# Attention with a soft mixture of experts and a gated layer: where the keys are rounded, and when the third pair's first maxima are taken

## The chip, the cores and the metric

The kernel runs on one core of one Trainium2 chip. The metric is the device time of one execution in microseconds (us). Engines are named as in the profile: PE is TensorE's matmul, PEld its weight load (which overlaps PE), DVE is VectorE, ACT is ScalarE, POOL is GpSimd, SP issues the DMAs.

## The reference, cut to what matters

```python
def _attn_ref(q, k, v):                       # q, k, v: 4 x 8 heads x 1152 x 64
    q_pool = q.reshape(B, H, S // 2, 2, D).mean(axis=3)          # 576 queries
    scores = scale * np.matmul(q_pool, k.transpose(0, 1, 3, 2))  # 576 x 1152
    scores = scores - np.max(scores, axis=-1, keepdims=True)
    attn = np.exp(scores)
    attn = attn / (np.sum(attn, axis=-1, keepdims=True) + 1e-09)
    return np.matmul(attn, v)
def reference(**kwargs):
    ...                                       # 2304 x 512 after the heads are put together
    x = _moe_ref(x=x, **moe_kwargs)           # soft mixture of 8 experts, 32 slots
    return _moe2_ref(x=x, **moe2_kwargs)      # RMS norm, gated layer of width 1536
```

The change concerns the attention alone.

## The kernel before

**Pairs.** The 32 heads are worked off as 16 pairs (`p` 0 to 15), one after the other; the two heads of a pair lie in the two halves of the 128 partitions. Everything else (experts, gated layer) comes after the last pair, apart from weights that are fetched and unpacked along the way.

**One pair.** There are 9 key tiles of 128 keys. For each, `qk` (L398) forms the scores of 288 queries in a two-bank tile `sc` in PSUM: four products per head, with keys and queries split into a rounded part and a rest (`kh`, `kl`, `qh`, `ql`), the fourth product subtracting the row maxima (`mr`). ACT takes the exponential (L409, tile `e`), POOL adds the exponentials up (`add_e`, L424, tile `acc`), and `av` (L426) multiplies them by the values. The row maxima have to be known beforehand, so they are computed one pair ahead: `max_item` (L319), for all but the first pair `wide_item` (L340), does products of the rounded parts alone into a two-bank tile `mxp`, and DVE reduces each tile to its maxima (L351, L357, L361, L364). A pair has 11 such items: 0 to 7 are four query tiles by two blocks of 512 keys, 8 takes the last 128 keys of all four query tiles, 9 and 10 take the last 64 queries. `max_red` and `max_row` then join them and turn them into a row (L374, tile `mxt`) that two DMAs per head send into `mr`.

**Visits.** Three key tiles make a visit; in its last tile (`kt % 3 == 2`) the steps `a`, `b`, `c` do the products with the values for all three tiles, and the steps `m` put maxima between them. Pair 0 does its two query halves one after the other (18 steps `u`, six visits), the others both together (9 steps, three visits).

**How many maxima.** `MAX`, `MAX_0` and `MAX_1` say how many items may be taken in each step. Pair 0 takes what is left of its own (five) and all 11 of pair 1; its last visit has none. Pair 1 takes items 0 to 8 of pair 2 and then items 0 to 2 of pair 3, 12 in all: one in its second step, four, four and three in its visits. From pair 2 on a pair takes items 3 to 8 of the next pair and 0 to 2 of the one after (`AHEAD` is 3), nine in all, three per visit. Items 9 and 10 of the next pair (`max_tail`) come in the first visit. `STEP_1` has one more `m` than `STEP_V` for pair 1's four, and `AT_P1` sets `max_red` later in pair 1.

**PSUM.** `sc`, `mxp` and the small tiles (`sums`, `sumt`, `xl`, `mxt`) take turns in three two-bank buffers. A tile can begin only when the engine that reads the last but two has done so.

**Side work.** All else is placed by the table `AT` (and `AT_0`, `AT_1`, ... for some pairs): a number is a point in the pair's 9 steps at which the function is written into the program, and each engine works through its instructions in the order in which they were written. Those of the first visit that matter here are `round_k` (L285: ACT rounds 576 keys of the pair after next, `kh` from `kraw`, whose DMA L275 is issued at the start of the pair), `abs_64` (ACT unpacks a weight, L714 and L716), `sums` (L446: PE sums up the exponentials' totals, ACT copies them to `srow`, L458), `max_tail`, and `recips` (L460: PE transposes `srow` into `sumt`, DVE takes reciprocals, L472).

Of the kernel before, what the change touches and what calls it, by code (L numbers as in the profile page):

```python
# [18 lines left out]
NP = 16  # L19
# [10 lines left out]

STEP = "q0 m q1 m e0 e1".split()
STEP_V = "q0 q1 m e0 e1 a m m b c".split()
STEP_1 = "q0 q1 m e0 e1 a m m b m c".split()
STEP_0 = "q e".split()
STEP_0V = "q e m a m m b m c".split()
VISIT = 3
PART = 5, 6
MAX = [0, 0, 3, 0, 0, 3, 0, 0, 3]
MAX_1 = [0, 1, 4, 0, 0, 4, 0, 0, 3]
NMAX = 9  # L40
AHEAD = 3
AT = dict(
    take_x=0.0,
    load_64=[0.1, 3.0, 5.0],
    load_q=0.3,
    load_k=0.31,
    spill=[1.4, 4.4],
    sum_q=2.2,
    round_k=[2.5, 5.5],
    abs_64=[2.51, 2.89, 8.5],  # L50
    sum_up=[0.1, 0.11],
    sums=2.75,
# [13 lines left out]
    max_red=5.75,  # L66
# [18 lines left out]
AT_0 = dict(  # L85
    load_v=7.3,
    round_k1=[0.6, 1.6],
    block_q1=1.62,
    low_q=2.1,
    row_0=2.97,  # L90
    low_k=[3.6, 5.1],
    load_q=4.3,
    load_k=5.73,
    sum_q=5.91,
    high_q=6.19,
    max_red=7.3,
    max_row=7.48,
    send_row=7.49,
    round_k=[7.6, 8.6],
    block_q=8.95,  # L100
)
AT_01 = dict(
    x_turn=8.85,
    x_divide=[8.86, 8.87],
    drop_x=8.88,
    d_exp=8.84,
)
AT_1 = dict(AT_01, turn_64=[0.9, 5.8, 5.81])
AT_P1 = dict(max_red=5.83)
AT_15 = dict(  # L110
    x_turn=5.8,
    x_divide=[5.81, 5.82],
# [1 line left out]
    sums_a=8.55,  # L114
    inverse_a=[8.56, 8.57],
)
MAX_0 = [0, 0, 4, 0, 0, 4, 0, 0, 3, 0, 0, 3, 0, 0, 2, 0, 0, 0]
HALVED = (0,)
SQ_DVE = (0, 2)
SP_ACT = (1, 5, 4, 3, 2)  # L120
# [28 lines left out]
def attention_softmoe_gated_kernel(ctx: ExitStack, tc: tile.TileContext, kT, qT, vv, ip, cst, w1, w2, wg, wv, wo, rg, out):  # L149
# [78 lines left out]
    def two_banks(name):  # L228
        return ps.tile([128, 2, 512], F32, tag="u", bufs=3, name=name)
# [110 lines left out]
    def wide_item(p, i):  # L340

        o = two_banks("mxp")
        q, k, m = qh[p], kh[p], mx3[p]
        heads = m[:, 0:2 * NQT].rearrange("p (s t) c -> p s t c", s=2)
        rest = slice(1024, 1152)
        if i < 8:
            t, c = divmod(i, 2)
            for s in range(2):
                r = slice(64 * s, 64 * s + 64)
                pe.matmul(o[:, s, :], lhsT=q[r, 128 * t:128 * t + 128], rhs=k[r, 512 * c:512 * c + 512], start=True, stop=True)  # L350
            dv.reduce_max(out=heads[:, :, t, c], in_=o, axis=AX.X)  # L351
        elif i == 8:
            for t in range(NQT):
                for s in range(2):
                    r = slice(64 * s, 64 * s + 64)
                    pe.matmul(o[:, s, 128 * t:128 * t + 128], lhsT=q[r, 128 * t:128 * t + 128], rhs=k[r, rest], start=True, stop=True)
            dv.reduce_max(out=heads[:, :, :, 2], in_=o.rearrange("p s (t k) -> p s t k", t=NQT), axis=AX.X)  # L357
        elif i == 9:
            for c in range(2):
                pe.matmul(o[:, c, :], lhsT=tb, rhs=k[:, 512 * c:512 * c + 512], start=True, stop=True)  # L360
            dv.reduce_max(out=m[:, 2 * NQT, 0:2], in_=o, axis=AX.X)  # L361
        else:
            pe.matmul(o[:, 0, 0:128], lhsT=tb, rhs=k[:, rest], start=True, stop=True)
            dv.reduce_max(out=m[:, 2 * NQT, 2:3], in_=o[:, 0:1, 0:128], axis=AX.X)  # L364
# [3 lines left out]
    def max_red(p):  # L368
        dv.reduce_max(out=mxw[:, 0:2 * NQT + 1], in_=mx3[p], axis=AX.X)
# [357 lines left out]
    def side(p):  # L727
        n, m, l = p + 1, p + 2, p - 1
        todo = []

        def at(name, g):
            ts = (AT_0 if p == 0 else AT_15 if p == NP - 1 else AT_P1 if p == 1 else AT if p % 4 == 3 else AT_1 if p % 4 == 1 else AT_01).get(name, AT.get(name))
            for i, t in enumerate(ts if isinstance(ts, list) else [ts]):
                todo.append((t, len(todo), (lambda i=i: g(i))))

        if p == 0:
            at("round_k1", lambda i: round_k(1, i))
            at("block_q1", lambda i: block_q(1))
            at("row_0", lambda i: (max_row(0), send_row(0, 3)))
        if n < NP:  # L740
            at("low_k", lambda i: low_k(n, slice(576 * i, 576 * i + 576)))
            at("low_q", lambda i: low_q(n))
            at("load_v", lambda i: load_v(n))
            if p:
                at("max_tail", lambda i: max_item(n, NMAX + i))
            at("max_red", lambda i: max_red(n))
            at("max_row", lambda i: max_row(n))
            at("send_row", lambda i: send_row(n))
        if m < NP:
            at("load_q", lambda i: load_q(m))  # L750
            at("load_k", lambda i: load_k(m))
            at("sum_q", lambda i: sum_q(m))
            at("high_q", lambda i: high_q(m))
            at("block_q", lambda i: block_q(m))
            at("round_k", lambda i: round_k(m, i))
        if l >= 0:
            at("take_x", lambda i: take_x(l))
            at("sum_up", lambda i: sum_up(l, 1 - i))
            at("sums", lambda i: sums(l))
            at("recips", lambda i: recips(l))  # L760
            at("x_turn", lambda i: x_turn_all(l))
            at("x_divide", lambda i: x_divide(l, range(3 * i, 3 * i + 3)))
            at("drop_x", lambda i: rel("B"))
            at("inverse", lambda i: inverse(l, i))
            at("x_logits", lambda i: x_logits(l))
            at("logit_add", lambda i: logit_add(l))
            if p % 4 == 0 and p < NP - 1:
                at("d_turn", lambda i: dpart.__setitem__(("d", l // 4), (d_turn(l // 4), d_neg(l // 4))))
                at("d_exp", lambda i: d_exp(l // 4, *dpart.pop(("d", l // 4))))
            if p % 4 == 1 and p > 1:  # L770
                b = p // 4 - 1
                at("d_back", lambda i: d_back(b))
                at("d_copy", lambda i: d_copy(b))
                at("slot_part", lambda i: slot_part(b))
                at("slot_copy", lambda i: slot_copy(b))
                at("slot_turn", lambda i: slot_turn(b, pt[:, b]))
            if p % 4 == 2 and p > 2:
                b = p // 4 - 1
                at("c_turn", lambda i: c_turn(b))
            if p % 4 == 3 and p > 3:  # L780
                b = p // 4 - 1
                at("c_exp", lambda i: c_exp(b))
                at("c_soft", lambda i: (c_sum, c_guard, c_inverse, c_out)[i](b))
        if p == 2:
            at("pair_up", lambda i: pair_up())
        if 0 < p < NP - 2:
            at("load_64", lambda i: load_64() if i < 2 or p % 2 or p < 11 else None)
            at("load_ew", lambda i: load(1, 99, KEEP_C + min(len(doubles), 4 * HELD + HELD_O)) if p >= FIRST_EW else None)
        if p < NP - 1:
            at("spill", lambda i: spill())  # L790
            at("abs_64", lambda i: abs_64(1))
            at("turn_64", lambda i: turn_64(1))
        if p == NP - 2:
            spill()
            assert not doubles
            at("load_14", lambda i: (keep_b.__setitem__(0, KEEP[3]), load(1, KEEP_A[0])))
        if p == NP - 1:
            at("sums_a", lambda i: sums(p))
            at("inverse_a", lambda i: inverse(p, i))
            at("load_15", lambda i: (keep_b.__setitem__(0, KEEP[0]), load(1, KEEP_A[1])))  # L800
        return sorted(todo, key=lambda x: x[:2])

    with tc.manual_schedule():
        q0 = qraw[0] = A([128, 2, 576], F32, "qraw")
# [46 lines left out]
        def next_max(p, mx):  # L851
            if p == 0:
                mx += 9
                if mx < 14:
                    max_item(0, mx)
                    if mx == 13:
                        max_red(0)
                else:
                    max_item(1, mx - 14)
            elif p == 1:  # L860
                max_item(2 + mx // NMAX, mx % NMAX)
            else:
                mx += AHEAD
                max_item(p + 1 + mx // NMAX, mx % NMAX)

        for p in range(NP):
            todo = side(p)
            mx = 0
            steps = [(kt, h) for h in range(2) for kt in range(NKT)] if p in HALVED else [(kt, None) for kt in range(NKT)]
            for u, (kt, h) in enumerate(steps):  # L870
                now = u / 2 if p in HALVED else u
                if kt % VISIT < VISIT - 1:
                    order = STEP if h is None else STEP_0
                else:
                    order = STEP_0V if p == 0 else STEP_1 if p == 1 else STEP_V
                quota = min(sum((MAX_0 if p == 0 else MAX_1 if p == 1 else MAX)[:u + 1]),
                            0 if p == NP - 1 else NMAX - AHEAD if p == NP - 2 else 99)
                for i, step in enumerate(order):
                    while todo and todo[0][0] <= now + i / len(order) / len(steps) * 9:
# [31 lines left out]
        for i in range(3):  # L911
            for s in range(2):
                c = slice(64 * s, 64 * s + 64)
# [196 lines left out]
        for h in range(2):  # L1110
            c = slice(256 * h, 256 * h + 256)
# [195 lines left out]
```

## Time and profile before

| | us |
|---|---|
| median of 3 runs | 722.66 (722.62 to 724.99) |
| the profiled execution | 725.93 |
| its span, first to last instruction | 723.8 |
| PE busy in the span | 692.3 (96%) |
| DVE, ACT, POOL busy | 459.5, 393.1, 435.3 |
| mean granted TensorE clock | 0.988 of full speed |

The three runs' times were taken without a profile; the rows below come from the profiled execution alone, which took 3.27 us more than their median and 2.13 us more than its own span. Busy PE includes matmuls that overlap, so it is read by stretch: how long a visit takes, and which wait stands inside it.

### The profile page before, as it was taken

What the parts mean: (1) busy time and instruction counts of PE and PEld (TensorE: products, weight loads), DVE (VectorE), ACT (ScalarE), POOL (GpSimd) and SP (SyncE); (2) the same over time, 40 slices, a digit from 0 to 9 for tenths busy, and PEclk for the clock granted to TensorE, in tenths of its full rate; (3) what the DMA queues carried; (4) which work ended last, traced back from release to release, by engine and by line L of the source; (5) the groups of instructions that cost most, each with busy time, mean ns of one, the idle gap of its engine ahead of it and who ended that gap; (6) DMA issues with size and microseconds to landing.
All of it is one profiled execution on the core that took longest, in us unless ns stands there. A gap on an engine that the chain in (4) does not pass through costs nothing.

```text
span 723.8 us, 15142 instructions
## 1 busy us (share of the span) xinstructions
PE 692.3 (96%) x5924; PEld 482.5 (67%) x5924; DVE 459.5 (63%) x663; ACT 393.1 (54%) x828; POOL 435.3 (60%) x352
## 2 busy tenths in 40 slices
PE   4998999999999999999999999879999999999998
PEld 2555676566676666666666666434467888888887
DVE  5748678887787878778878775531155755534420
ACT  2454666657657666566766545442266865554320
POOL 5585787877687867687887676230036855535320
PEclk9999999999999999999999999979999999999999
DMA  5140634834736626436427407379980100000001
GB/s 178 52 179 24 212 102 131 263 114 158 240 132 207 212 83 239 163 142 244 139 95 242 138 15 265 118 278 393 381 316 0 44 15 29 30 30 29 15 34 40
DMA packets 52854, 103.54 MB, mean 143 GB/s; under 512 B 5816, under 2 KB 19632, under 8 KB 52784
## 3 DMA queue, kind: packets, MB, share of 16 engines
q1 hardware_dynamic: 52784, 102.59, 40.9%
q8 instruction: 46, 0.75, 0.4%
q14 instruction: 24, 0.20, 0.1%
HBM read 89.39 MB, written 13.11 MB: 142 GB/s over the span
## 4 chain that ended last, share of the span: by engine, by line
PE 85%; DMA 6%; DVE 3%; ACT 3%; issue 2%; POOL 0%; SPq 0%; ACTq 0%; DVEq 0%; POOLq 0%
PE yo L1210 21%; PE sc L407 20%; PE av L430 20%; PE mxp L350 4%; PE gv L1162 4%; DMA kraw<-in_kT_dram 3%; DMA w<-away 2%; PE hin L976 2%; PE xo L492 2%; PE so L999 2%; PE xl L509 1%; PE sums L455 1%; PE mxp L360 1%; PE x L1027 1%; PE pp L569 1%
## 5 line engine op out<-in xcount | busy, mean ns | idle before, releaser
L424 POOL TENSOR_TENSOR acc<-acc,e 128x576 f32<-128x576 f32 x154 | 216.4, 1425 | 44.5 <-ACT e L409 40.3
L409 ACT ACTIVATE e<-sc 128x576 f32<-128x576 f32 x288 | 164.2, 657 | 71.0 <-PE sc L407 70.4
L351 DVE TENSOR_REDUCE mx<-mxp 128x2 f32<-128x1024 f32 x120 | 143.9, 1223 | 67.1 <-PE mxp L350 66.7
L430 PE MATMUL av<-e,vt 128*64 128x288 f32 x1152 | 168.7, 418 | 0.2 <-ACT e L409 0.2
L424 POOL TENSOR_TENSOR acc<-e 128x576 f32<-128x576 f32 x63 | 93.6, 1495 | 74.7 <-ACT e L409 74.6
L430 PEld LDWEIGHTS av<-e,vt 128*64 128x64 f32 x1152 | 72.2, 136 | 64.4 <-issue 29.6
L1210 PE MATMUL yo<-woh,hA 128*128 128x512 f32 (+1 forms) x312 | 98.9, 384 | 0.0
L407 PE MATMUL sc<-qh,kh 64*128 64x288 f32 x576 | 94.3, 324 | 1.4 <-DVE mx L351 1.0
L407 PE MATMUL sc<-mr,pick 64*128 64x288 f32 x576 | 86.6, 297 | 0.0
L407 PE MATMUL sc<-ql,kh 64*128 64x288 f32 x576 | 86.3, 296 | 0.0
L407 PE MATMUL sc<-qh,kl 64*128 64x288 f32 x576 | 86.3, 296 | 0.0
L1167 DVE SCALAR_TENSOR_TENSOR th<-th,gv 128x384 f32<-128x384 f32 x72 | 39.8, 553 | 63.0 <-ACT th L1164 62.4
L1193 POOL TENSOR_TENSOR hA<-hu,hA 128x384 fp32r<-128x384 f32 x48 | 48.7, 1016 | 42.6 <-ACT hA L1192 38.9
L407 PEld LDWEIGHTS sc<-qh,kh 64*128 64x128 f32 x576 | 55.3, 189 | 20.9 <-issue 6.6
L1210 PEld LDWEIGHTS yo<-woh,hA 128*128 128x128 f32 x312 | 57.6, 188 | 10.2 <-issue 0.7
L1164 ACT ACTIVATE th<-gv 128x384 f32<-128x384 f32 x72 | 35.2, 489 | 42.4 <-PE gv L1162 39.1
L1210 PE MATMUL yo<-wol,hA 128*128 128x512 f32 (+1 forms) x151 | 57.8, 383 | 0.0
L407 PEld LDWEIGHTS sc<-qh,kl 64*128 64x128 f32 x576 | 55.7, 190 | 0.0
L407 PEld LDWEIGHTS sc<-mr,pick 64*128 64x128 f32 x576 | 55.5, 189 | 0.0
L407 PEld LDWEIGHTS sc<-ql,kh 64*128 64x128 f32 x576 | 55.3, 188 | 0.0
L350 PE MATMUL mxp<-kh,qh 64*128 64x512 f32 x240 | 47.6, 434 | 0.0
L1169 DVE SCALAR_TENSOR_TENSOR hu<-th,gv 128x384 f32<-128x384 f32 x72 | 39.9, 554 | 8.0
(191 smaller groups left out, 1041.4 us busy)
## 6 DMA issues: line engine op xcount, KB each, us to landing
w<-in_w_dram SPq DMA_DIRECT2D x86, 256.0 KB
w<-in_w_dram SPq DMA_DIRECT2D x21, 512.0 KB
vt<-in_vv_dram SPq DMA_DIRECT2D x16, 576.0 KB
qraw<-in_qT_dram SPq DMA_DIRECT2D x15, 576.0 KB
kraw<-in_kT_dram SPq DMA_DIRECT2D x15, 576.0 KB
away<-w SPq DMA_DIRECT2D x32, 256.0 KB
w<-away SPq DMA_DIRECT2D x32, 256.0 KB
raw<-in_wg_dram SPq DMA_DIRECT2D x12, 512.0 KB
```

What stands on the lines that cost most here:

```text
L350: pe.matmul(o[:, s, :], lhsT=q[r, 128 * t:128 * t + 128], rhs=k[r, 512 * c:512 * c + 512], start=True, stop=True)
L351: dv.reduce_max(out=heads[:, :, t, c], in_=o, axis=AX.X)
L407: pe.matmul(o[:, s, 0:HQ], lhsT=w[r, wk], rhs=q[r, c], start=(i == 0), stop=(i == 3))
L409: ac.activation(ets[p, kt, h], o[:, :, 0:HQ], AF.Exp, scale=0.0625)
L424: eng.tensor_tensor(out=acc[p, h, j], in0=first[p, h, j] if n == 1 else acc[p, h, j], in1=e, op=ALU.add)
L430: pe.matmul(avt[p, h][64 * s:64 * s + 64, 0:HQ], lhsT=vt[p][:, kt, 64 * s:64 * s + 64], rhs=ets[p, kt, h][:, s], start=(kt == 0), stop=(kt ...
L1162: pe.matmul(o[i], lhsT=sg[n][:, 256 * i + 128 * c:256 * i + 128 * c + 128], rhs=cT[g], start=True, stop=True)
L1164: ac.activation(t, o[0], AF.Tanh, scale=0.5)
L1167: dv.scalar_tensor_tensor(out=t, in0=t, scalar=1.0, in1=o[0], op0=ALU.add, op1=ALU.mult)
L1169: dv.scalar_tensor_tensor(out=u, in0=t, scalar=0.5, in1=o[1], op0=ALU.mult, op1=ALU.mult)
L1193: gp.tensor_tensor(out=b, in0=u, in1=f(a), op=ALU.subtract)
L1210: pe.matmul(o, lhsT=x, rhs=w[:, c], start=(ft == 0 and i == 0), stop=(ft == NF - 1 and i == 2))
```

## The change

Three edits. First, the first half of the keys (576 of 1152) of the pair after next is no longer rounded at 2.5 of the pair's steps but at 2.88, in pairs 1 to 13: behind the first unpacked weight, the copy of the sums, `d_copy` where there is one, the two `max_tail` items and the transposes of the sums, and ahead of the second unpacked weight (2.89). Second, items 0 to 2 of pair 2 are taken in pair 0's last visit, so that pair 1 takes nine items like every later pair; `STEP_1`, `MAX_1` and `AT_P1` go, and pair 1 is placed by `AT`. Third, items 0 to 7 run over the query tiles first and the key blocks second, in all pairs, so that items 0 to 3 read keys 0 to 511 alone, which lie in the first rounded half.

```diff
-STEP_1 = "q0 q1 m e0 e1 a m m b m c".split()
-MAX_1 = [0, 1, 4, 0, 0, 4, 0, 0, 3]
-    round_k=[2.5, 5.5],
+    round_k=[2.88, 5.5],
-AT_P1 = dict(max_red=5.83)
-MAX_0 = [0, 0, 4, 0, 0, 4, 0, 0, 3, 0, 0, 3, 0, 0, 2, 0, 0, 0]
+MAX_0 = [0, 0, 4, 0, 0, 4, 0, 0, 3, 0, 0, 3, 0, 0, 2, 0, 0, 3]
         if i < 8:
-            t, c = divmod(i, 2)
+            c, t = divmod(i, 4)
...
-                    max_item(1, mx - 14)
-            elif p == 1:
-                max_item(2 + mx // NMAX, mx % NMAX)
+                    i = mx - 14
+                    max_item(1 + i // 11, i % 11)
...
-                    order = STEP_0V if p == 0 else STEP_1 if p == 1 else STEP_V
-                quota = min(sum((MAX_0 if p == 0 else MAX_1 if p == 1 else MAX)[:u + 1]),
+                    order = STEP_0V if p == 0 else STEP_V
+                quota = min(sum((MAX_0 if p == 0 else MAX)[:u + 1]),
```

ACT at the end of pair 4's first visit, before: behind the six exponentials come the rounded keys, a weight (two instructions), the copy of the sums and a second weight.

```order
L409 ACTIVATE e<-sc 128x576 x6
L289 CAST kh<-kraw 128x576
L714 ACTIVATE w_1839<-raw_1540 128x512
L716 ACTIVATE raw_1540<-raw_1540 128x512
L458 ACTIVATE srow<-sums 128x288
L714 ACTIVATE w_1874<-raw_1745 128x512
L716 ACTIVATE raw_1745<-raw_1745 128x512
L409 ACTIVATE e<-sc 128x576 x6
```

The same place now (the lines of the changed file are three lower).

```order
L406 ACTIVATE e<-sc 128x576 x6
L711 ACTIVATE w_1837<-raw_1540 128x512
L713 ACTIVATE raw_1540<-raw_1540 128x512
L455 ACTIVATE srow<-sums 128x288
L286 CAST kh<-kraw 128x576
L711 ACTIVATE w_1874<-raw_1745 128x512
L713 ACTIVATE raw_1745<-raw_1745 128x512
L406 ACTIVATE e<-sc 128x576 x6
```

The rounding has moved behind the first weight and the copy of the sums, and stands ahead of the second weight and of the next visit's exponentials.

PE from the end of pair 0 to pair 1's second step, before: the last products of scores of pair 0, six with the values, and three score tiles of pair 1 (four rows each, of which `mr,pick` is the last) with a maximum behind them.

```order
L407 MATMUL sc<-mr_82,pick_85 128x288 x2
L430 MATMUL av<-e,vt 64x288 x6
L407 MATMUL sc<-qh,kh 128x288 x2
...
L407 MATMUL sc<-mr_83,pick_84 128x288 x2
L350 MATMUL mxp<-kh,qh 128x512 x2
L407 MATMUL sc<-qh,kh 128x288 x2
```

The same place now.

```order
L404 MATMUL sc<-mr_82,pick_85 128x288 x2
L347 MATMUL mxp<-kh,qh 128x512 x2
L427 MATMUL av<-e,vt 64x288 x2
L347 MATMUL mxp<-kh,qh 128x512 x4
L427 MATMUL av<-e,vt 64x288 x4
L404 MATMUL sc<-qh,kh 128x288 x2
...
L404 MATMUL sc<-mr_83,pick_84 128x288 x2
L347 MATMUL mxp<-kh,qh 128x512 x2
```

Three maxima stand between pair 0's products with the values, and pair 1's first six score tiles follow one another without one.

## Rows read from the trace of the kernel before

**Rows 1.** The page: busy time and share of the span, by engine.
```profile
PE 692.3 (96%) x5924; PEld 482.5 (67%) x5924; DVE 459.5 (63%) x663; ACT 393.1 (54%) x828; POOL 435.3 (60%) x352
```

**Rows 2.** Stretches: start:end, length, busy us by engine, PEclk, DMA share, GB/s.
```profile
29.39:33.81 4.42, 4.42 (x43) 2.72 (x43) 3.96 (x5) 1.73 (x3) 2.78 (x2) 1.00 0.19 23
...
43.32:47.16 3.84, 3.69 (x37) 2.23 (x36) 0.00 (x0) 3.25 (x7) 2.52 (x2) 1.00 0.01 1
47.16:59.46 12.30, 10.79 (x98) 6.42 (x96) 9.01 (x11) 6.68 (x14) 8.98 (x7) 1.00 0.64 225
59.46:70.75 11.29, 9.32 (x93) 6.14 (x91) 9.16 (x11) 4.97 (x10) 6.94 (x5) 1.00 0.01 2
70.75:80.72 9.97, 9.97 (x85) 7.26 (x84) 5.36 (x7) 5.55 (x10) 6.93 (x5) 0.83 0.60 192
80.72:90.11 9.39, 9.39 (x94) 6.12 (x92) 7.05 (x10) 7.03 (x14) 6.65 (x5) 1.00 0.59 192
90.11:98.56 8.45, 8.45 (x92) 6.10 (x90) 7.02 (x11) 4.97 (x10) 6.93 (x6) 1.00 0.06 22
98.56:107.03 8.47, 8.47 (x85) 5.78 (x84) 6.73 (x9) 5.30 (x10) 8.21 (x9) 1.00 0.50 155
72.00:74.00 2.00, 2.00 (x22) 2.00 (x20) 0.00 (x0) 1.38 (x3) 1.40 (x1) 0.50 0.02 2
256.78:266.12 9.34, 9.34 (x91) 7.00 (x89) 5.34 (x8) 5.13 (x10) 6.96 (x5) 0.89 0.05 18
```

**Rows 3.** Timeline of pair 1, PEld and DVE: start, length, instruction, idle before.
```profile
51.58 0.19 PEld L407 LDWEIGHTS sc<-qh,kh 64*128 64x128 f32 x2 [1.19 <-DVE mx L351]
...
70.50 0.14 PEld L374 LDWEIGHTS mxt<-cs,mxw 128*128 128x128 f32 x1 [2.40 <-issue]
...
68.95 1.21 DVE L357 TENSOR_REDUCE mx<-mxp 128x8 f32<-128x1024 f32 x1
```

**Rows 4.** Timeline of pair 0's last visit, PEld and ACT.
```profile
45.13 0.20 PEld L430 LDWEIGHTS av<-e,vt 128*64 128x64 f32 x4 [0.16 <-issue]
...
44.72 0.67 ACT L289 CAST kh<-kraw 128x576 fp32r<-128x576 f32 x1
```

**Rows 5.** Timeline of ACT at the end of pair 4's first visit; last row pair 9's.
```profile
141.37 0.67 ACT L289 CAST kh<-kraw 128x576 fp32r<-128x576 f32 x1 [3.27 <-DMA kraw<-in_kT_dram]
...
143.06 0.40 ACT L458 ACTIVATE srow<-sums 128x288 f32<-128x288 f32 x1
...
146.13 0.65 ACT L409 ACTIVATE e<-sc 128x576 f32<-128x576 f32 x1 [1.53 <-PE sc L407]
...
285.86 0.65 ACT L409 ACTIVATE e<-sc 128x576 f32<-128x576 f32 x1 [1.44 <-PE sc L407]
```

**Rows 6.** Who waited for whom: us in total, times, longest.
```profile
ACT kh L289 <- DMA kraw<-in_kT_dram: 11.3, 6, 3.3
...
PEld mxp L363 <- ACT srow L458: 5.5, 4, 2.2
```

**Rows 7.** Timeline: item 9's reduction, next visit's first scores, pairs 4, 6, 8, 12.
```profile
141.79 1.23 DVE L361 TENSOR_REDUCE mx<-mxp 128x2 f32<-128x1024 f32 x1 [0.27 <-PE mxp L360]
...
145.23 0.19 PEld L407 LDWEIGHTS sc<-qh,kh 64*128 64x128 f32 x2 [0.44 <-DVE ql L308]
...
199.46 1.22 DVE L361 TENSOR_REDUCE mx<-mxp 128x2 f32<-128x1024 f32 x1 [0.28 <-PE mxp L360]
...
200.86 0.19 PEld L407 LDWEIGHTS sc<-qh,kh 64*128 64x128 f32 x2 [0.44 <-DVE mx L361]
...
252.75 1.23 DVE L361 TENSOR_REDUCE mx<-mxp 128x2 f32<-128x1024 f32 x1 [0.27 <-PE mxp L360]
...
256.78 0.29 PEld L407 LDWEIGHTS sc<-qh,kh 64*128 64x128 f32 x2 [0.86 <-DVE ql L308]
...
365.21 1.23 DVE L361 TENSOR_REDUCE mx<-mxp 128x2 f32<-128x1024 f32 x1 [0.27 <-PE mxp L360]
...
367.25 0.19 PEld L407 LDWEIGHTS sc<-qh,kh 64*128 64x128 f32 x2 [0.44 <-DVE rr L472]
```

More of the change, by code (lines that the diff above doesn't have):

```diff
@@ L731, in at @@
         def at(name, g):
-            ts = (AT_0 if p == 0 else AT_15 if p == NP - 1 else AT_P1 if p == 1 else AT if p % 4 == 3 else AT_1 if p % 4 == 1 else AT_01).get(name, AT.get(name))
+            ts = (AT_0 if p == 0 else AT_15 if p == NP - 1 else AT if p == 1 or p % 4 == 3 else AT_1 if p % 4 == 1 else AT_01).get(name, AT.get(name))
             for i, t in enumerate(ts if isinstance(ts, list) else [ts]):
```

## The prediction, made before the changed kernel had run

> **What bounds the kernel now.** I read the page first. PE is busy for 692.3 of 723.8 us, 96%, and no other engine comes over 67% [rows 1]: the products set the time, and the change neither adds nor removes one. It can pay only where PE stands still or runs slowly. So I read next how long each pair, and each visit in it, takes, from one visit's first weight load for scores to the next one's, and compared pairs that do the same work. Pair 1 is the odd one: its three visits take 12.30, 11.29 and 9.97 us, pair 2's take 9.39, 8.45 and 8.47 [rows 2]. That is 33.56 against 26.31 us. Pair 1 has twelve maxima items where pair 2 has nine, but its PE is busy for 10.79 and 9.32 us only in the first two visits: most of the excess is waiting.
>
> The timeline of pair 1 says for what. At 51.58 PE has waited 1.19 us for a reduction (L351) to give back a PSUM buffer: the item in pair 1's second step holds one of three buffers, and DVE comes to it late. At 70.50 PE has stood for 2.40 us ahead of the transpose of the maxima (L374), which needs the reduction of item 8; that began only at 68.95 and took 1.21 [rows 3]. Right behind this wait the granted clock is 0.50, TensorE's lower level of 1.2 GHz, and the third visit runs at 0.83 on average [rows 2]: this is why it takes 9.97 us with PE busy throughout.
>
> The list of waits shows the second place. ACT waits six times for keys in `round_k`, 11.3 us in all, and PE waits four times, 5.5 us in all, for the copy of the sums (L458) before item 10 may use its buffer (L363) [rows 6]. In pair 4 the two are one: ACT stands 3.27 us at `round_k`, which begins when its DMA lands at 141.37, and the copy of the sums, third behind it, comes at 143.06 [rows 5]. Pairs 8 and 12 look alike.
>
> **The maxima.** Nothing is added: the change moves three items of two products and one reduction each.
>
> What pair 0's last visit pays. It takes 3.84 us without maxima; pair 0's visit from 29.39, the same work with three, takes 4.42 [rows 2]. So at least 0.58. Two things come on top. The first item needs the first half of the rounded keys, and ACT rounds them from 44.72 for 0.67, to 45.39; the products with the values, in whose place the item now stands, begin at 45.13 [rows 4]. That is 0.26 of waiting, which I put at about 0.27. And the three reductions take some 1.2 each, one after the other (as L357's 1.21 [rows 3]), so that the third is done about 3.7 us behind the first item, some 0.3 after pair 1's third score tile wants its buffer (an estimate). Together 1.15, with 0.58 as the lower end and about 1.5 as the upper (all of a reduction's 1.2 left over, less what the old visit already waited).
>
> What pair 1 gets back. With nine items, the order of the later pairs and keys that are there, it does what pair 2 does, so I take pair 2's visits: 12.30 - 9.39 = 2.91, 11.29 - 8.45 = 2.84, 9.97 - 8.47 = 1.50, together 7.25 [rows 2]. The lower end is the two named waits and the clock alone: 1.19 + 2.40 + 1.50 = 5.09 [rows 2, 3]. The upper end is 7.25, since nothing in pair 1 is lighter than in pair 2. The new order of items 0 to 7 changes which weights each product loads, not how many loads there are; I cost it at nothing in the other pairs.
>
> **The rounding.** 13 instructions of 0.67 us [rows 5] move behind the copy of the sums; ACT's work stays the same. What remains late then? In pair 6, where PE does not wait for the sums, item 9's reduction ends at 199.46 + 1.22 = 200.68 and the next visit's scores begin 0.18 later [rows 7]: this reduction gives back the buffer and sets the start. It does not depend on the sums. So the next visit starts 0.18 behind it in the others too:
>
> - pair 4: 141.79 + 1.23 + 0.18 = 143.20 instead of 145.23, a gain of 2.03;
> - pair 8: 252.75 + 1.23 + 0.18 = 254.16 instead of 256.78, a gain of 2.62;
> - pair 12: 365.21 + 1.23 + 0.18 = 366.62 instead of 367.25, a gain of 0.63 [all rows 7].
>
> Pair 8's next visit takes 9.34 us at a mean clock of 0.89, where pair 2's takes 8.45 at 1.00 [rows 2]: without the wait before it I count the clock's 0.89 as well. Sum 6.17. The fourth of the waits is small and I leave it out. Ends: 0, if the wait only changes its victim, and about 6.5.
>
> The moved wait has new neighbours. Behind `round_k` on ACT now stand a second weight and the six exponentials of the next visit. In pair 4 it still begins at 141.37; with the weight behind it, as long as the three instructions up to 143.06, ACT is free at about 143.06. The first exponential is wanted when its scores are there, 0.90 behind the visit's start (146.13 - 145.23 [rows 5, 7]), at 143.20 + 0.90 = 144.10. A margin of 1.04 us hides it. In pairs whose keys are there in time the rounding simply comes 0.67 later; the shortest idle time of ACT ahead of a first exponential among pairs 2 to 14 is 1.44 [rows 5], so these lose nothing. POOL and SP issue the same instructions in the same order; the DMA of the keys is issued as before, relative to its pair.
>
> A rule of the Trainium skill speaks against this edit ("TensorE: Matmul & The Clock Gate", the table at its head): ScalarE's queue is strictly first in, first out. So whatever waits on ACT keeps waiting what stands behind it, exponentials too; by that rule alone the wait is moved, not removed, and its 3.27 us in pair 4 would have to be paid by the exponentials. The row of pair 4 agrees that ACT passes nothing by, as the copy of the sums shows; the margin above decides, not the rule.
>
> **Sum.** +1.15 - 7.25 - 6.17 = -12.27 us. Against the profiled execution that is 725.93 - 12.27 = 713.7. The median of the runs lies 3.27 lower; what the profile costs is unknown, and I take the same difference there: 722.66 - 12.27 = 710.4, 1.7% less. What follows the last pair shifts as a whole, since pairs 14 and 15 and their transfers stay as they are.
>
> **The rivals.**
>
> *The clock is not given back.* 1.50 + 0.89 = 2.39 of the sum is time at the lower clock [rows 2]. It may be that the unprofiled runs have no such stretch, or that other waits lower the clock once everything comes earlier. For: one of the three runs took 2.3 us more than the other two, and pair 4's wait is about as long as pair 8's, yet only pair 8's is followed by a slow visit. Against: the largest waits of the attention go. Then 722.66 - 9.88 = 712.8; with both effects 715. The Trainium skill (the same page, part 1 on the clock gate) says that the window over which activity is judged runs freely and does not start with the kernel. By that rule the same wait may cost clock in one version and not in another; the difference between pairs 4 and 8 agrees with it.
>
> *The rounding gives nothing.* If the keys land about a microsecond later than now, relative to their pair, the exponentials pay what the sums paid. For: the 11.3 us of waiting for keys stay. Against: the margin of 1.04. Then 722.66 + 1.15 - 7.25 = 716.6.
>
> *The maxima give nothing.* If pair 1 is held up by something other than its items (POOL's sums come late at its start, DVE is busy for 9.01 of 12.30 us), only the rounding pays: 722.66 - 6.17 = 716.5, or 717.6 with pair 0's cost.
>
> *Slower.* The moved wait stands ahead of the exponentials in 13 pairs. It decides from the point where keys land over 1.04 us later than in pair 4; beyond, each microsecond is paid in full by PE. To eat up 12.27 us each of 13 pairs must lose 0.94, so the landing has to be 2.0 us later in every one. At 2.5 us it is 13 x 1.46 = 19.0, and the kernel takes 729. Against: only pairs 4 and 8 land as late, and the DMA's place in its queue is unchanged.
>
> **How the numbers follow.** The forecast 710.4 (707.5 to 712.5 by the bounds of its terms) has a chance of 0.62; the clock's rival at 712.8 (up to 715) 0.16; the rounding without gain 0.09; the maxima without gain 0.07; slower 0.03; and 0.03 that hardly anything moves. The range that holds 8 in 10 reaches from 706.5, where the terms stand at their better ends and a slow stretch after the attention goes as well, to 716.5, into the two partial cases. What a measurement can tell from no change is about 0.5%, 3.6 us, that is 719.0 to 726.3. Faster by more: 0.92; within: 0.05; slower by more: 0.03.
>
> **What would show it.** Right: pair 1 takes about 26.6 us in the profile after, with no wait over 1 us in it and the clock at 1.00; PE's waits for the copy of the sums are gone from the list; pairs 4, 8 and 12 start their second visit about 9.4 us after their first; ACT still waits for keys, some 11 us in all, and the first exponential waits for scores, not the scores for exponentials. Wrong: waits of PE for exponentials at the start of second visits (the rounding's rival), a wait of several microseconds at pair 1's start for reductions of pair 2's maxima (pair 0's cost is too small), or the lower clock in other pairs.

## The result, and the profile after

| | before, us | after, us |
|---|---|---|
| median of 4 runs | 723.33 (722.62 to 724.99) | 714.74 (714.48 to 715.36) |
| the profiled execution | 725.93 | 714.64 |
| its span | 723.8 | 712.8 |
| end of the last pair's exponentials | 459.83 | 447.54 |

The medians differ by 8.6 us, or 1.2%; the ratio on record is 0.9864 with the interval 0.9843 to 0.9885, in which the medians' own 0.9881 lies too. The forecast was 710.4, 12.3 us less. The profiled execution of the changed kernel is one of its four runs; that of the kernel before is none of its four and lies above them all. Between these two executions the difference is 11.3 us, and within the attention it is 12.29, almost to the hundredth what the sum said. That near agreement is partly luck, as the account below shows term by term. So the reading of this one trace was right in the main, and what it stands for was not quite: that is what most of the experiments are about.

The stretches of the profile after, from one visit's first weight load for scores to the next one's (start:end, length, busy us of PE, PEld, DVE, ACT, POOL, then PEclk, DMA share, GB/s): pair 0's last visit, pair 1's three visits, pair 4's first, pair 8's first and second, pair 12's first.

```profile
43.00:47.97 4.97, 4.74 (x44) 2.81 (x44) 2.31 (x3) 3.90 (x9) 3.58 (x3) 1.00 0.11 20
47.97:57.48 9.51, 9.51 (x95) 6.10 (x94) 7.50 (x10) 6.13 (x11) 7.34 (x6) 1.00 0.78 281
57.48:66.24 8.76, 8.71 (x93) 6.13 (x91) 7.00 (x11) 4.97 (x10) 6.87 (x6) 1.00 0.01 3
66.24:74.54 8.30, 8.30 (x86) 5.86 (x86) 6.39 (x8) 5.28 (x10) 6.93 (x6) 1.00 0.52 170
127.42:136.80 9.38, 9.38 (x94) 6.12 (x92) 7.89 (x11) 7.17 (x14) 7.32 (x6) 1.00 0.96 312
236.66:246.05 9.39, 9.39 (x94) 6.13 (x93) 7.90 (x11) 7.02 (x14) 7.34 (x6) 1.00 1.00 331
246.05:254.49 8.44, 8.44 (x92) 6.10 (x90) 7.52 (x11) 4.98 (x10) 7.42 (x6) 1.00 0.30 105
345.59:354.97 9.38, 9.38 (x95) 6.13 (x93) 7.89 (x11) 7.02 (x14) 7.32 (x6) 1.00 0.91 287
```

Against [rows 2]: pair 0's last visit went from 3.84 to 4.97, pair 1's from 12.30, 11.29 and 9.97 to 9.51, 8.76 and 8.30, its clock is at 1.00 throughout, and PE is busy in it without a hole to speak of. The first visits of pairs 4, 8 and 12 are all alike, 9.38 or 9.39. In the profile before they were these:

```profile
133.81:145.23 11.42, 9.66 (x94) 6.06 (x93) 9.02 (x13) 7.02 (x14) 8.01 (x6) 1.00 0.98 326
244.79:256.78 11.99, 10.27 (x95) 6.16 (x93) 9.65 (x13) 7.02 (x14) 8.04 (x6) 0.94 0.95 321
357.24:367.25 10.01, 9.64 (x95) 6.05 (x93) 8.53 (x12) 7.03 (x14) 7.96 (x6) 1.00 0.86 283
```

ACT at the end of pair 4's first visit (timeline after: start, length, instruction, idle before), against [rows 5]:

```profile
133.71 0.41 ACT L455 ACTIVATE srow<-sums 128x288 f32<-128x288 f32 x1 [0.88 <-PE sums L452]
134.58 0.68 ACT L286 CAST kh<-kraw 128x576 fp32r<-128x576 f32 x1 [0.46 <-DMA kraw<-in_kT_dram]
135.17 0.68 ACT L711 ACTIVATE w<-raw 128x512 f32<-128x512 f32 x1
135.75 0.67 ACT L713 ACTIVATE raw<-raw 128x512 int32<-128x512 uint16 x1
137.71 0.65 ACT L406 ACTIVATE e<-sc 128x576 f32<-128x576 f32 x1 [1.28 <-PE sc L404]
```

The copy of the sums comes as soon as PE has the sums, the rounding waits 0.46 for its keys behind it, and ACT still idles 1.28 us ahead of the first exponential, for scores. Item 9's reduction on DVE, and the next visit's first weight load, in the same place:

```profile
135.40 1.22 DVE L358 TENSOR_REDUCE mx<-mxp 128x2 f32<-128x1024 f32 x1 [0.27 <-PE mxp L357]
```
```profile
136.80 0.19 PEld L404 LDWEIGHTS sc<-qh,kh 64*128 64x128 f32 x2 [0.44 <-DVE mx L358]
```

The reduction ends at 136.62, and the visit starts 0.18 behind it, as the forecast said.

What follows the last pair did not shift as a whole. This stretch, before and then after:

```profile
459.83:723.78 263.95, 250.80 (x1613) 186.56 (x1609) 108.47 (x218) 120.75 (x295) 97.42 (x99) 0.98 0.33 120
```
```profile
447.54:712.79 265.25, 252.27 (x1613) 187.30 (x1609) 108.47 (x218) 120.72 (x294) 97.56 (x99) 0.97 0.33 120
459.10:469.20 10.10, 9.09 (x64) 4.79 (x62) 2.94 (x11) 2.80 (x6) 2.44 (x2) 0.50 0.61 209
```

It takes 1.30 us more, with the same number of PE's instructions, and the clock stands at 0.50 for ten microseconds on end behind the first waits of this part. In the profile before that stretch was shorter, but a later profile of the kernel before (724.88 us in all) has one as long, and there the whole part took 264.90 us:

```profile
473.91:480.74 6.83, 6.07 (x44) 3.51 (x44) 1.54 (x4) 2.57 (x6) 3.27 (x3) 0.50 0.92 338
```
```profile
470.85:481.09 10.24, 9.69 (x70) 5.74 (x66) 2.19 (x7) 2.87 (x6) 3.75 (x3) 0.50 0.81 288
```

So the longer stretch does not come with the change alone.

### The profile page after: what moved, and what is told of

It reads as the page before. It is cut to its first block, busy times and chain, and to the rows that moved or that the text cites. A ratio compares the mean times of both kernels' runs of the same rounds, so it can differ in the third digit from the quotient of the medians.

```text
span 712.8 us, 15141 instructions
## 1 busy us (share of the span) xinstructions
PE 688.8 (97%) x5924; PEld 481.2 (68%) x5924; DVE 460.2 (65%) x663; ACT 392.8 (55%) x828; POOL 435.8 (61%) x352
## 4 chain that ended last, share of the span: by engine, by line
PE 90%; DMA 3%; DVE 2%; ACT 2%; issue 2%; POOL 1%; SPq 0%; DVEq 0%; ACTq 0%; POOLq 0%
PE sc L404 22%; PE av L427 21%; PE yo L1206 21%; PE mxp L347 5%; PE gv L1158 4%; DMA w<-away 2%; PE hin L972 2%; PE xo L489 2%; PE so L995 1%; PE xl L506 1%; PE sums L452 1%; PE mxp L357 1%; PE pp L566 1%; PE mxp L353 1%; PE c4o L1016 1%
## 5 line engine op out<-in xcount | busy, mean ns | idle before, releaser
L1206 PEld LDWEIGHTS yo<-woh,hA 128*128 128x128 f32 x312 | 57.6, 188 | 10.2 <-issue 0.7
```

What stands on the lines that cost most here:

```text
L1206: pe.matmul(o, lhsT=x, rhs=w[:, c], start=(ft == 0 and i == 0), stop=(ft == NF - 1 and i == 2))
```

## The experiments

**The two halves of the change, each alone.** The first kernel is the one before with one number changed:

```diff
-    round_k=[2.5, 5.5],
+    round_k=[2.88, 5.5],
```

> The kernel before with the rounding of the keys at 2.88 and nothing else. My theory (the wait for the keys is hidden there): in the profile pairs 4, 8 and 12 have first visits of about 9.4 us, pair 8's second visit takes 8.45, PE's waits for the copy of the sums are gone, pair 1 still takes about 33 us; attention ends about 6.2 us earlier than in the profile of before (about 453.6 instead of 459.8), and the timed median falls by 4 to 6 us. Rival (the rounding only moves the wait): the time stays within 1 us of before, and the first exponentials of the second visits come late.

The second is the changed kernel with that number put back:

```diff
-    round_k=[2.88, 5.5],
+    round_k=[2.5, 5.5],
```

> The changed kernel with the rounding put back to 2.5, so that only the maxima move and are put in the new order. My theory: pair 0's last visit takes about 1.1 us more, pair 1 takes about 26.7 to 27 us, the later pairs take what they took before, pairs 4, 8 and 12 with first visits of 11.4, 12.0 and 10.0; attention ends 6 us earlier, and the timed median falls by 4 to 6 us. Together with the rounding alone this adds up to the whole change. Rival (the maxima give nothing, pair 1 is held up by something else): pair 1 stays above 31 us.

Timed in the same rounds, the kernel before took 724.32 us (722.12 to 727.51, 11 runs), the rounding alone 719.70 (719.24 to 722.77, 6 runs; ratio 0.9939, 0.9916 to 0.9962) and the maxima alone 719.74 (716.52 to 720.81, 6 runs; 0.9925, 0.9899 to 0.9951). Each gives 4.6 us, and the two add up to 9.2; the whole change gave 8.6 in its first rounds and 9.65 in later ones (below). The stretches of the rounding alone, pair 1 and then the first visits of pairs 4, 8 and 12:

```profile
47.12:80.71 33.59, 30.09 (x274) 19.85 (x272) 23.53 (x27) 17.18 (x33) 22.85 (x17) 0.95 0.41 136
133.57:142.96 9.39, 9.39 (x96) 6.13 (x94) 7.90 (x11) 7.14 (x14) 7.35 (x6) 1.00 0.94 311
242.51:251.89 9.38, 9.38 (x95) 6.13 (x94) 7.90 (x11) 7.12 (x14) 7.33 (x6) 1.00 1.00 322
351.44:360.83 9.39, 9.39 (x96) 6.13 (x94) 7.90 (x11) 7.01 (x14) 7.34 (x6) 1.00 0.89 300
```

And of the maxima alone, pair 1 and the first visits of pairs 4 and 8:

```profile
48.42:74.98 26.56, 26.52 (x267) 18.09 (x265) 20.89 (x26) 16.31 (x31) 21.17 (x16) 1.00 0.45 152
127.86:138.33 10.47, 9.66 (x94) 6.05 (x92) 8.93 (x12) 7.01 (x14) 8.06 (x6) 1.00 0.94 314
238.18:250.03 11.85, 10.12 (x94) 6.11 (x92) 9.49 (x13) 7.03 (x14) 8.06 (x6) 0.96 0.93 306
```

Each half cures its own place and leaves the other. Both rivals fall. But with the maxima alone pair 4's first visit, 10.47, is not the 11.42 of the first profile, and pair 12's is 9.38, not 10.01: the place that the rounding cures is not equally bad every time. The maxima alone are still two edits, the moved items and the new order of items 0 to 7; no run tells these two apart. One of the six runs of the rounding alone took 722.77, some 3 us more than the rest; why is open.

**The same kernels again.** Four more profiles of the two kernels, unchanged, to see what varies:

> The kernel before, unchanged, profiled once more. The median of the change is 8.6 us, my sum and the two profiles say 11 to 12. My theory: the stretches at the lower clock fall differently from execution to execution, so in this profile pair 1's third visit (9.97 us in the first profile) or pair 8's second (9.34) may be at full clock, near 8.5, and the whole time then is 1 to 3 us under the first profile's 725.93. Rival (a profile costs a fixed amount, the timed runs differ only in not being profiled): the same stretches are slow and the time is 725.9 again.

> The kernel before, profiled again. My theory: what differs from the first two profiles of it is ACT's waiting for keys (11.3 and 6.4 us there) and with it the first visits of pairs 3, 4, 8 and 12 (10.0, 11.4, 12.0, 10.0 in the first, 9.8, 10.9, 10.2, 9.4 in the second); attention ends between 455 and 461, later the more ACT waits. Pair 1 takes 33 to 34 us in every one. Rival (only the clock differs): these four visits take the same as in one of the two.

> The same once more, with the same expectations: attention ends between 455 and 461 and follows ACT's waiting for keys in pairs 3, 4, 8 and 12; all other pairs repeat to 0.3 us.

> The changed kernel, unchanged, profiled once more. My theory: the pairs take the same times within 0.3 us, attention ends at 447.5 again, and what differs is where the clock is low after the attention; the time is 714.5 to 715.4. Rival: the attention itself varies by over 1 us.

The first visits of pairs 4, 8 and 12 in two of these profiles of the kernel before, the quickest and the longest (721.66 and 726.61 us):

```profile
133.43:144.33 10.90, 9.65 (x94) 6.06 (x92) 9.02 (x13) 7.03 (x14) 8.08 (x6) 1.00 0.97 324
243.89:254.08 10.19, 9.67 (x94) 6.05 (x92) 8.70 (x12) 7.05 (x14) 8.07 (x6) 1.00 1.00 327
353.63:363.01 9.38, 9.38 (x96) 6.13 (x94) 7.90 (x11) 7.04 (x14) 7.33 (x6) 1.00 0.88 294
```
```profile
133.95:145.16 11.21, 9.67 (x95) 6.06 (x93) 9.02 (x13) 7.02 (x14) 8.02 (x6) 1.00 0.95 316
244.74:256.42 11.68, 9.87 (x96) 6.06 (x94) 9.24 (x13) 7.03 (x14) 8.02 (x6) 0.98 0.97 317
357.67:367.79 10.12, 9.66 (x94) 6.05 (x92) 8.62 (x12) 7.04 (x14) 8.07 (x6) 1.00 0.84 283
```

Read the three lengths of each against 9.38, what these visits take once the keys don't matter: 2.33 us too long in the quick one, 4.87 in the long one. With pair 3 and pair 8's second visit, the four pairs' excess over the lengths they have after the change is 6.4, 2.3, 3.8 and 6.1 us in the four profiles of the kernel before, in the order in which they were taken. In the last two pair 9's first visit was 0.4 us too long as well (10.2 instead of 9.8), against the expectation that all other pairs repeat to 0.3. Pair 1 took 33.56, 33.39, 33.56 and 33.60: that loss is there every time, with its stretch at the lower clock (0.50 in all four). Pair 8's stretch at 0.50 is there in two of four. Attention ended at 459.83, 455.58, 457.87 and 460.40, a mean of 458.42. That it ends later the more ACT waits for keys did not hold: ACT waited 11.3, 6.4, 11.2 and 9.8 us; the ends follow the excess of the visits, not the sum of the waits. My theory for the first repeat, that the clock makes the difference, was mostly wrong: the time fell by 4.27 us, the excess by 4.1, and of that 0.9 was pair 8's stretch at 0.50, the rest the first visits. In the changed kernel's repeats attention ended at 447.58 and 448.49, and all that differs in them by more than 0.1 us is the length of pair 0's first two visits together (12.9 to 13.7, also in other kernels). The rival of a fixed cost of profiling falls: one profiled execution took 721.66, and in the timed runs whose span is on record the time lies as far above the span (723.49 against 721.4) as in the first profiled execution (725.93 against 723.8).

**The changed kernel timed beside the kernel before.**

> The changed kernel, timed beside the one above and the kernel before. My theory: its runs lie within 1 us of one another (714.4 to 715.4), those of before spread over 3 to 5 us, since only in the latter the landing of the keys reaches the path; the ratio is 0.984 to 0.989. Rival (the spread is the clock's alone): both spread alike.

714.89 us (714.41 to 715.54, 5 runs) against 724.54 (721.84 to 726.98, 9 runs); ratio 0.9867, 0.9845 to 0.9890. The changed kernel's runs lie within 1.1 us of one another, those of before within 5.1. The means of the profiles roughly agree: attention ends 458.42 - 447.87 = 10.55 us earlier (447.87 is the mean of the three profiles of the changed kernel), and what follows takes 0.8 us more (four profiles of before 264.23 on average, three of after 265.01), which leaves 9.8, against the 9.65 measured.

The expectation's reason for the spread fits the profiles, in which the excess of the visits goes from 2.3 to 6.4 us as the time goes from 721.66 to 726.61. It is not the whole of it, as the one long run of the rounding alone (722.77) shows.

**How late may the keys come?** The sharpest test of the margin that the forecast gave the moved wait: the DMA of the keys is issued later on purpose, first behind two expert weights (1.2), then behind the stores of unpacked weights too (1.5, in the changed kernel and in the kernel before).

```diff
-    load_k=0.31,
+    load_k=1.2,
```
```diff
-    load_k=0.31,
+    load_k=1.5,
```

> The changed kernel with the DMA of the keys issued behind two expert weights of 256 KB each (its point moves from 0.31 to 1.2 of the pair's steps; in pairs 4 to 13 the two stand between). At the 340 GB/s of a full stretch that is some 1.5 us later (an estimate). My theory (a margin of 1.04 us hides the wait for the keys in front of the exponentials): only pairs whose keys land latest, 4 and 8, lose up to 0.5 us each; attention ends at 447.5 to 449.5. Rival (no margin, every delay is paid): ten pairs lose 1.5 each and attention ends at 460 or later.

> The changed kernel with the DMA of the keys issued still later, at 1.5, behind the stores of unpacked weights as well, which wait for DVE some 3.5 us into the pair. The keys then land some 11 to 12 us after the pair's start instead of about 7. My theory: the margin is used up, ACT stands in front of the exponentials, and pairs 3 to 13 lose 2 to 4 us each in their second visits; attention ends 20 to 40 us later, 467 to 487. Rival (the exponentials have slack enough, or other transfers give way): under 5 us later.

> The kernel before with the same late DMA of the keys (1.5). My theory: here the rounding holds up the copy of the sums and with it the next visit's start, so that the same lateness costs 1 to 2 us per pair more than in the changed kernel; PE's waits for the copy of the sums come in most pairs, 30 us or more in all. Attention ends 10 us or more behind that of the changed kernel with the same DMA. Rival (the order on ACT makes no difference): both ends are 12 us apart or less only by what the maxima give, about 6.

The first of the three tested nothing of the margin. SP issued the keys that pair 4 rounds as before, 0.11 us behind the pair's start (127.42 in the profile after, 129.46 here). Only the two expert weights had gone ahead of them:

```profile
127.53 0.34 SPq L272 DMA_DIRECT2D kraw<-in_kT_dram  x1
```
```profile
129.57 0.33 SPq L272 DMA_DIRECT2D kraw<-in_kT_dram  x1
```

The same holds in pairs 3, 8 and 12. So the issue "at the start of the pair" is not true of every pair: in the profile after, the keys that pairs 3, 4, 5, 8, 9 and 12 round go out 0.11 us behind the pair's start, and those that pairs 6, 7, 10, 11 and 13 round some 4.5 us ahead of it. The six waits for keys in [rows 6] all lie in pairs whose keys go out behind the start, though pair 5, such a pair too, had none. With 1.2 no rounding at L286 waited for keys, and pairs 1 to 15 took the same times as without; attention ended at 449.58 because pair 0's scores began 1.06 us later (17.23 instead of 16.17) and its first two visits took 13.9 us instead of 12.9.

With 1.5 the issue did move: pair 4's keys went out 3.79 us behind the pair's start. The changed kernel took 716.34 us in all, the kernel before 761.11. The waits, in the changed kernel and then in the kernel before (us in total, times, longest):

```profile
ACT kh L286 <- DMA kraw<-in_kT_dram: 13.7, 9, 2.2
```
```profile
ACT kh L289 <- DMA kraw<-in_kT_dram: 47.3, 13, 5.5
...
PEld mxp L363 <- ACT srow L458: 28.4, 9, 4.4
```

The same late issue costs 36.1 us of attention in the old order (it ends at 495.89 instead of 459.83) and 1.1 in the new (448.65 instead of 447.54), and in both some 0.8 of that lies in pair 0. The lateness of the landing is not the same: in the old order the keys landed at up to 9.8 us behind the pair's start (9.30 in pair 4, against 8.44 in the new), so a part of the 36.1 is that. My expectation for the changed kernel was far off: the keys did not land 11 to 12 us behind their pair's start but at 7.8 to 9.4 where they were waited for, since they took less time from issue to landing (4.65 us in pair 4, instead of 7.05 in the profile after), and the margin took nearly all of it. The one pair over the margin is pair 3. Its ACT, and then its second visit:

```profile
110.96 0.67 ACT L286 CAST kh<-kraw 128x576 fp32r<-128x576 f32 x1 [2.21 <-DMA kraw<-in_kT_dram]
...
112.67 0.64 ACT L406 ACTIVATE e<-sc 128x576 f32<-128x576 f32 x1
```
```profile
111.45:120.19 8.74, 8.69 (x92) 6.11 (x90) 7.03 (x11) 6.17 (x13) 6.92 (x6) 1.00 0.18 60
```

The exponential begins at 112.67 right behind the moved work, where its scores allowed 111.45 + 0.90 = 112.35: 0.32 late, and the visit takes 8.74 instead of 8.44. In this one pair the delay beyond the margin is paid in full, as the forecast's slower case said; in the eight others that waited nothing is paid.

**Rounding pair 2's keys earlier in pair 0.** In the changed kernel PE waits for them ahead of the first of the moved maxima:

```profile
45.11 0.19 PEld L347 LDWEIGHTS mxp<-kh,qh 64*128 64x128 f32 x2 [0.47 <-ACT kh L286]
```

So this half was moved ahead of the row of maxima, where ACT stands idle (in `AT_0`, the table of pair 0):

```diff
-    round_k=[7.6, 8.6],
+    round_k=[7.45, 8.6],
```

> The changed kernel with the first half of pair 2's keys rounded earlier in pair 0, at 7.45 instead of 7.6, ahead of the row of maxima, where ACT stands idle. My theory: PE's wait for the keys ahead of the first of the moved maxima (0.47 us, estimated 0.27 in the prediction) goes, and with it some 0.4 to 0.8 us of pair 0's last visit (9.69 with the two visits' half before it); attention ends 0.4 to 0.8 earlier. Rival (the exponentials set the pace there): nothing moves, since the next maxima wait for an exponential anyway.

> The changed kernel with pair 2's keys rounded at 7.45 in pair 0, now timed. My theory: the 0.49 us that pair 0's last visit lost in the profile is all there is; the median is 0.3 to 0.7 us under that of the changed kernel timed beside it (714.0 to 714.5). Rival: lost in the spread of the runs, no difference over 0.2 us.

Pair 0's last visit in the first of these:

```profile
43.16:47.62 4.46, 4.46 (x43) 2.76 (x42) 2.30 (x3) 3.40 (x8) 3.63 (x3) 1.00 0.05 8
```

4.46 instead of 4.97: PE no longer stands still in it. Timed, 714.36 us (714.05 to 714.63) against 714.89 (714.41 to 715.54) of the changed kernel in the same rounds. The medians differ by 0.53, which agrees with the 0.5 of the profile. The profile shows the gain; the times alone do not, since the two sets of runs overlap a little and the length of pair 0's first two visits alone varies by more (12.9 to 13.9). Against the kernel before: 0.9860, 0.9838 to 0.9882. By its median this is the quickest version that was run.

## Why the prediction was right, and where it was off

**Pair 0 pays 1.15.** It paid 1.13 (4.97 - 3.84). Of its parts the wait for the keys was 0.47 instead of 0.27. The one for the reductions, put at 0.3, was 0.15 us ahead of pair 1's third score tile, and so stands in pair 1's 9.51 and not in the 4.97. The sum came out right because one part was too small and the other was paid elsewhere: luck in the number, the mechanism as forecast.

**Pair 1 gets back 7.25.** It got 6.99 in the profile (33.56 - 26.57) and 6.8 to 7.0 against any profile of the kernel before. The second visit stayed 0.31 over pair 2's: one score tile waits 0.29 for the first exponential, which comes 1.2 us behind the visit's start instead of 0.9. Pair 1 had this wait before the change too, and the forecast, which named two waits and the clock, did not see it. Before, then after:

```profile
61.37 0.19 PEld L407 LDWEIGHTS sc<-qh,kh 64*128 64x128 f32 x2 [0.28 <-ACT e L409]
```
```profile
59.39 0.19 PEld L404 LDWEIGHTS sc<-qh,kh 64*128 64x128 f32 x2 [0.29 <-ACT e L406]
```

So pair 1 does not do quite what pair 2 does. Pair 6's second visit has such a wait only since the change (8.72 instead of 8.44): it is there with the maxima alone and absent with the rounding alone. That one belongs to the maxima, against the forecast's "at nothing in the other pairs". Why the exponential is late in these two pairs and no others is open.

**The rounding gives 6.17.** The mechanism was right to the hundredth: the next visit's start 0.18 us behind item 9's reduction gave 9.39 for pair 4, and 9.38 was measured. As a forecast of the median this is the mis-sized term. It was read from an execution in which the keys landed late in all of pairs 3, 4, 8 and 12. Over four profiles of the kernel before, what it could give was 6.4, 2.3, 3.8 and 6.1 us, 4.7 on average, and the timed runs of the rounding alone gave 4.6 (by its interval 2.8 to 6.1).

**The agreement within the attention.** The 12.29 us between the two profiles are 6.99 of pair 1 and 6.36 of the rounding (6.17, and 0.19 of pair 3 that the forecast left out), less 1.13 in pair 0's last visit and 0.28 in pair 6, and 0.32 by which pair 0 came to its last visit earlier (43.00 instead of 43.32). The last has nothing to do with the change. So the terms hold to about 0.3 us each, and the 0.02 between 12.27 and 12.29 is luck.

**The step to the median failed.** "I take the same difference there" made the sum of one execution the sum of all. The difference of 3.27 between the profiled execution and the median was not a cost of the profile that both kernels share. About half of it was the very loss that the change removes, 6.4 us in this execution against 4.7 on average, so that a smaller sum belonged to the smaller time. The other half is that the median of three was low: in later rounds the kernel before had medians of 724.32 and 724.54, not 722.66. Against the profiled execution the same sum gave 713.7, and the changed kernel's profiled execution took 714.64.

**The range.** The lower bound, 707.5, does not follow from the terms: their better ends add up to 0.58 - 7.25 - 6.5 = -13.17, which is 709.5. The measured 714.74 lies above the 712.5 that the terms were to allow, in the part of the wide range that was kept for a half of the change giving nothing. Neither half gave nothing; the step to the median brought it there. That the range holds it is luck in part.

**What follows the last pair** was said to shift as a whole. It took 1.3 us more in the profile after, with the clock lower for longer behind its waits. On average it took 0.8 more, but the four profiles of before (263.95 to 264.90) and the three of after (264.57 to 265.25) overlap, and one of the former has the same long stretch. Whether the change causes it is not shown. It is the forecast's rival of the clock, in another place than the one it was sought in: pair 1's stretch was given back in full, in every profile.

**What the profile after should show.** Pair 1 at 26.6 with nothing over 1 us waiting and a full clock: so it was. PE's waits for the copy of the sums ahead of item 10 are gone, and the second visits of pairs 4, 8 and 12 start 9.4 us after the first. "ACT still waits for keys, some 11 us in all" was wrong: it waited 0.46, since the rounding's turn now comes behind the sums, 6.6 us or more into the pair, when most keys have landed.

**The slower case** put its point at keys landing 1.04 us later than pair 4's, that is 8.60 behind the pair's start. With the late DMA pair 4 rounded at 8.44 and had 0.02 us of idle time left ahead of the exponential: the point is there, within 0.15. Landing so late did not occur in the changed kernel by itself.

## What to carry to other kernels

Where an engine works through its instructions in the order written, as ACT did here, a wait holds up what stands behind it; so put the instruction that may wait behind the short one that others need, where the engine would idle anyway, and work out from the rows how late it may come. A loss that comes from a transfer's landing differed here from one execution to the next: before a sum read from one profile is set against a median, see whether that profile was a long one, and for which reason. A pair that does more of a repeated step than the others is found by comparing the lengths of equal stretches, and the lengths of its neighbours were a good forecast here of what it takes when it is made alike (26.31 forecast, 26.57 measured). And before a delay that was put in on purpose is taken as a test, see in the trace that the transfer was in fact issued later.

## What the runs showed of the hardware that was not expected

The keys of one pair, issued 0.1 us behind the pair's start every time, landed 7.5, 6.3, 7.1 and 7.6 us behind it in pair 8 of four executions of the same program, with the DMA engines busy for 95 to 100% of the first visit. In the changed kernel's three profiles they were there by 6.6 or landed at 7.1 to 7.2 in pairs 4 and 8; with pair 2's keys rounded earlier they landed at 7.5 in pair 8 of one profile. Whether the change makes them land earlier is not settled.

The wait of 2.4 us in pair 1 was followed by 0.50 of the clock in every one of four profiles, but the waits for the copy of the sums in pairs 4 and 8 in only two of eight cases, both in pair 8, after 2.15 and 2.23 us. Pair 4's waits of 2.19 and 1.98 us in the same two profiles were not followed by a lower clock. Pair 8's second visit took 9.34 and 9.72 us in these two cases, 8.43 in the others. With the maxima alone a wait of 2.16 us in pair 8 was followed by 0.50, and the second visit took 9.48. In the kernel before with the late DMA the second visits were at full clock behind longer waits, 3.03 us in pair 7 and 2.90 in pair 10. What decides between such near equal waits is open.
